# Query rows in seven units of 128, full-array scores and eleven value slots in an attention and maxout kernel

## The chip, the core and the metric

The kernel runs on one core of one Trainium2 chip. The metric is the device time of a whole execution, in microseconds (us). Of the core this text names TensorE (PE, its weight loads PEld), VectorE (DVE), ScalarE (ACT), GpSimd (POOL) and SyncE (SP). SP computes nothing here; it issues the DMAs, one after another and in program order.

## The reference

The inputs are q, k, v of shape (8, 12, 448, 64), that is 8 batches of 12 heads with 448 rows of 64, two gain vectors of 64, and four 768 x 768 weight matrices. All are float32 in the computation (the weights arrive as 64-bit floats, which the kernel decodes itself).

```python
def rmsnorm(x, g):
    rms = np.sqrt(np.mean(x * x, axis=-1, keepdims=True) + 1e-06)
    return x / rms * g
q_n, k_n = rmsnorm(q, g_q), rmsnorm(k, g_k)
scores = np.matmul(q_n, k_n.transpose(0, 1, 3, 2)) / np.sqrt(64)
attn = np.exp(scores - scores.max(-1, keepdims=True))
attn = attn / (attn.sum(-1, keepdims=True) + 1e-09)
x = np.matmul(attn, v)          # heads side by side: 3584 tokens x 768
h = np.maximum(np.maximum(x @ w1, x @ w2), x @ w3)
out = h @ w_out
```

## The kernel before

Work goes by pairs of heads: pair g of 48 holds two heads of one batch, six pairs make a batch. `beat(g, i)` is called with g from 0 to 48 and i from 0 to 11, so a pair has twelve beats, and each beat emits instructions of several stages for all engines. The order in which `beat` and what it calls emit them is the order in which each engine executes; nothing reorders them. Each emitted instruction waits on semaphores for its operands and buffers. An engine whose next instruction waits holds up all that is behind it.

The first six pairs (`PLAIN = 6`) are computed in float32. From pair 6 on each float32 operand of a product is split into an upper and a lower float16 part, and a product is three float16 products (upper by upper, upper by lower, lower by upper: `TERMS`).

A pair from 6 on goes through these steps:

- **Loads** (`load_q`, `load_k`, `load_v`; L332, L344 to L349), three pairs ahead for queries and keys (beats 0 and 1), six ahead for values (beat 5). Queries: 112 partitions, four rows of each head on a partition, one DMA for the pair. Keys and values: seven groups of 64 columns on 128 partitions, three of each head and one that holds the last 64 rows of one head on the lower half of the partitions and of the other head on the upper half; four DMAs for each of the two tensors.
- **Normalise** two pairs ahead: squares on POOL (L367), their sums on DVE (L374), power -0.5 on POOL (L388, L392), scale on POOL (L399, L411, L424, L428).
- **Split and transpose** one pair ahead: upper part on ACT (L439), lower on POOL (L445), then one DMA transpose each for keys and queries (`turn_rows`, L455): kt and qt have the head's 64 columns on partitions, head 0 on the lower half and head 1 on the upper.
- **Scores** (`scores`, L558): four query blocks of 112 rows (c = 0 to 3), each for both heads. A matmul has K = 64, one head on each half of the array's rows, so the two heads' matmuls run beside each other. Three terms make six matmuls of 448 columns in a block.
- **Softmax**: maximum over both heads in one DVE instruction (L569), exponential with sum on ACT for each head (L583), scaled upper part on ACT (L658), lower part on DVE (L668).
- **Transpose of the weights** (`turn_weights`, L678): one DMA transpose for each block into pt. The one of block 3 is emitted at beat 2 of the next pair, the others at beats 5, 8 and 11.
- **Weighted sum** (`add_values`, L706), at beat 7 of the next pair: output columns of the two heads on the two halves of the array, four groups of keys by three terms by two heads, 24 matmuls of 448 columns, which go by twos beside each other: 12 slots.

The plain pairs transpose on PE instead (`turn_whole` L468, `turn_plain` L605), so SP has only loads for them.

Between these, `thirds` feeds the feed-forward part of batches already attended to: 18 first-layer blocks of 18 matmuls of 448 columns (L735) and six or eight second-layer blocks of 18 matmuls of 384 columns (L799) for each batch. The quota of a beat (`THIRDS`) is fixed, so that one batch's feed-forward is spread over the next six pairs. That of the last batch runs after the last attention pair. Results are stored from SP (L774) by query block order: since four rows lie on a partition, a 128-token block is written in two pieces as a rule. The weights are loaded, decoded on DVE (L198, L202, L207) and split during the first twelve pairs or so.

Of the kernel before, what the change touches and what calls it, by code (L numbers as in the profile page):

```python
# [16 lines left out]
P = 128  # L17
# [22 lines left out]
def qknorm_attention_maxout_ffn_kernel(  # L40
# [41 lines left out]
    QP = S // NQ  # L82
# [51 lines left out]
    half_neg = const.tile([P, 15], F32, name="half_neg")  # L134
    nc.vector.memset(half_neg, -0.5)
    half = const.tile([P, 1], F32, name="half")
    nc.vector.memset(half, 0.5)

    sums = [const.tile([P, 15], F32, name=f"ss{i}") for i in range(2)]
    for t in sums:  # L140
        nc.vector.memset(t, 1.0)

    key_rows = [const.tile([P, 4, 2, D], F32, name=f"kn{i}") for i in range(2)]
    for t in key_rows:
        nc.gpsimd.memset(t[HALVES[1], 3, 0], 0.0)
        nc.gpsimd.memset(t[HALVES[0], 0, 1], 0.0)
# [181 lines left out]

    def load_q(g):
        b, pr = divmod(g, NP)  # L330
        qr = sb.tile([QP, 2, NQ, D], F32, name="qr", bufs=2)
        nc.sync.dma_start(  # L332
            out=qr,
            in_=q[b, 2 * pr:2 * pr + 2].rearrange("h (p c) d -> p h c d", c=NQ),
        )
        st.setdefault(g, {})["qr"] = qr


    def load_kv(g, name, src, bufs, on=(nc.sync, nc.sync)):
        b, pr = divmod(g, NP)  # L340
        t = sb.tile([P, 7, D], F32, name=name, bufs=bufs)
        rows = src[b, 2 * pr:2 * pr + 2]
        for h in range(2):
            on[h].dma_start(  # L344
                out=t[:, 4 * h:4 * h + 3],
                in_=rows[h, 0:3 * P].rearrange("(p c) d -> p c d", c=3),
            )
        on[0].dma_start(out=t[HALVES[0], 3], in_=rows[0, 3 * P:S])
        on[1].dma_start(out=t[HALVES[1], 3], in_=rows[1, 3 * P:S])  # L349
        st.setdefault(g, {})[name] = t  # L350

    def load_k(g):
        load_kv(g, "kr", k, 2, (nc.sync, nc.sync if g else nc.scalar))

    def load_v(g):
        load_kv(g, "vr", v, 8)


    def squares(g, what):
        s = st[g]  # L360
        src = s["kr"] if what == "k" else s["qr"].rearrange("p h c d -> p (h c) d")
        rows, n = src.shape[0], src.shape[1]
        sq = sb.tile([P, 8, D], F32, name="sq", tag="rows", bufs=3)[:rows, :n]
        if g < 2:
            nc.scalar.activation(sq, src, AF.Square)
        else:
            nc.gpsimd.tensor_tensor(out=sq, in0=src, in1=src, op=ALU.mult)  # L367
        s["sq" + what] = sq

    KQ = {"k": slice(0, 7), "q": slice(7, 15)}  # L370

    def sum_squares(g, what):
        sq = st[g].pop("sq" + what)
        nc.vector.tensor_reduce(  # L374
            sums[g % 2][:sq.shape[0], KQ[what]], sq, axis=AX, op=ALU.add
        )

    def inv_rms(g, what):
        s, at = st[g], KQ[what]
        if "ri" not in s:  # L380
            s["ri"] = sb.tile([P, 15], F32, name="ri", bufs=2).rearrange(
                "p (n o) -> p n o", o=1
            )
        ri = s["ri"][:, at, 0]
        by, eps = 1.0 / D, RMS_EPS
        if what == "k":
            by, eps = k_mean, k_eps
# [6 lines left out]
    def scale_q(g):  # L394
        s = st[g]
        qr, ri = s.pop("qr"), s.pop("ri")
        qn = sb.tile([QP, 4, 2, D], F32, name="qn", tag="rows", bufs=3)
        on = nc.gpsimd if g else nc.vector
        on.tensor_tensor(  # L399
            out=qn.rearrange("p c h d -> p h c d"),  # L400
            in0=qr,
            in1=ri[:QP, 7:].rearrange("p (h c) o -> p h c o", h=2).broadcast_to(
                [QP, 2, 4, D]
            ),
            op=ALU.mult,
        )
        s["qn"] = qn
        if g < PLAIN:
            return
        n = qn.rearrange("p c h d -> p (c h) d")  # L410
        nc.gpsimd.tensor_tensor(  # L411
            out=n, in0=n,
            in1=gain[:QP].rearrange("p (o d) -> p o d", o=1).broadcast_to([QP, 8, D]),
            op=ALU.mult,
        )

    def scale_k(g):
        s = st[g]
        kr, ri = s.pop("kr"), s["ri"]
        kn = key_rows[g % 2]  # L420
        on = nc.gpsimd if g else nc.vector
        for h, rows in enumerate(HALVES):
            own = slice(4 * h, 4 * h + 3)
            on.tensor_tensor(  # L424
                out=kn[:, h:h + 3, h], in0=kr[:, own],
                in1=ri[:, own].broadcast_to([P, 3, D]), op=ALU.mult,
            )
            on.tensor_tensor(  # L428
                out=kn[rows, 3 - 3 * h, h:h + 1], in0=kr[rows, 3:4],
                in1=ri[rows, 3:4].broadcast_to([64, 1, D]), op=ALU.mult,  # L430
            )
        s["kn"] = kn


    def upper_rows(g, what):
        s = st[g]
        n = s.pop(what + "n").rearrange("p c h d -> p (c h d)")
        parts = sb.tile([n.shape[0], 2, 4 * P], F16, name=what + "p", bufs=1)
        nc.scalar.copy(parts[:, 0], n)  # L439
        s[what + "p"] = parts, n  # L440

    def lower_rows(g, what):
# [3 lines left out]
            out=parts[:, 1], in0=n, in1=parts[:, 0], op=ALU.subtract  # L446
# [3 lines left out]
    def turn_rows(g, what):  # L450
        s = st[g]
        parts = s.pop(what + "p")
        rows = parts.shape[0]
        t = sb.tile([P, 2, 4, rows], F16, name=what + "t", bufs=2)
        nc.sync.dma_start_transpose(  # L455
# [630 lines left out]
```

## Time and profile before

| | us |
|---|---|
| median of three runs | 1091.29 (1090.59 to 1093.42) |
| the profiled execution | 1093.06 |
| its span, first to last instruction | 1091.2 |
| PE busy | 1008.7 (92%) |
| DVE, ACT, POOL busy | 760.4, 690.3, 714.8 |
| mean share of the DMA engines' time in use | 68.6% |

The profile is of one execution. Busy time of PE is that of pipelined matmuls whose ends are modelled, so a stretch of matmuls is read by the distance between starts. SP has no busy time on the page; its rows in the timeline (SPq) are the instructions that issue a DMA, and their length is how long the issue held SP, not how long the data took. "Landing" in the list of DMAs counts from the issue until the data is there. A merged row (x2, x3) runs from the first start to the last end and includes what lies between.

### The profile page before, as it was taken

Reading aid. Unit: us, or ns where it says so; the run is one execution under the profiler, and the core shown is the slowest. Engines: PE = TensorE matmul, PEld = TensorE weight load, DVE = VectorE, ACT = ScalarE, POOL = GpSimd, SP = SyncE. Lnnn points to the kernel's source line nnn. Section 1 sums busy time; section 2 is a strip of 40 time slices with the busy share of each in tenths; the row PEclk is TensorE's granted clock in tenths of the full one; section 3 lists DMA queues with packets and bytes.
Section 4 is the critical chain, followed back from the end, with each engine's and each line's share of the span. In section 5 each row is a group of like instructions: output and inputs, shape, how many; then the busy total and the mean of one; then the engine's idle time right before and its main releaser. Section 6 shows DMA issues by size and latency. Waiting matters only on the chain.

```text
span 1091.2 us, 18210 instructions
## 1 busy us (share of the span) xinstructions
PE 1008.7 (92%) x6168; PEld 497.0 (46%) x6168; DVE 760.4 (70%) x1395; ACT 690.3 (63%) x1575; POOL 714.8 (65%) x806
## 2 busy tenths in 40 slices
PE   3576868988899999999999999999999999999998
PEld 1333333434444454444544454444444554445555
DVE  3799998898767686786777767777686766761210
ACT  3488878757767576676766676667676676752001
POOL 5378898966777778677777776777777777610000
PEclk9698777999999999999999999999999999999999
DMA  4544458776798779888887798878877797653002
GB/s 127 172 144 155 146 152 177 163 146 124 156 174 146 145 156 177 155 154 139 177 150 145 142 169 173 152 138 160 173 151 137 142 183 137 112 98 73 1 1 58
DMA packets 426652, 152.27 MB, mean 140 GB/s; under 512 B 372928, under 2 KB 422336, under 8 KB 426560
## 3 DMA queue, kind: packets, MB, share of 16 engines
q1 hardware_dynamic: 425888, 150.75, 68.6%
q8 instruction: 48, 0.79, 0.3%
q10 hardware_dynamic: 672, 0.38, 0.1%
q14 instruction: 44, 0.36, 0.1%
HBM read 51.97 MB, written 11.01 MB: 58 GB/s over the span
## 4 chain that ended last, share of the span: by engine, by line
PE 69%; DVE 4%; ACT 2%; issue 2%; DVEq 0%; ACTq 0%
PE acc L735 37%; PE acc L799 14%; PE sc L558 9%; PE av L706 9%; DVE pp L668 2%; ACT pp L658 1%; DVE nm L569 1%; DVE wo_sb L314 0%; ACT xt L720 0%; ACT wo_sb L309 0%; DVE acc L749 0%; DVE ht L759 0%; DVE v_rows L172 0%; ACT ht L755 0%; ACT kp L439 0%
## 5 line engine op out<-in xcount | busy, mean ns | idle before, releaser
L735 PE MATMUL acc<-xt,w_sb 128*128 128x448 f16 x2592 | 518.4, 355 | 0.0
L735 PEld LDWEIGHTS <-w_sb 128*128 128x128 f16 x2592 | 244.6, 98 | 260.3 <-issue 49.8
L583 ACT ACTIVATE sc<-sc,nm 112x448 f32<-112x448 f32 x336 | 204.2, 608 | 191.0 <-DVE nm L569 184.4
L569 DVE TENSOR_REDUCE nm<-sc 112x2 f32<-112x896 f32 x192 | 208.2, 1084 | 94.2 <-PE sc L558 92.8
L658 ACT ACTIVATE pp<-sc,rs 112x448 f16<-112x448 f32 x336 | 195.1, 633 | 63.7 <-ACT sc L583 32.5
L668 DVE SCALAR_TENSOR_TENSOR pp<-sc,rs,pp 112x448 f16<-112x448 f32 x336 | 212.7, 674 | 1.6 <-ACT pp L658 1.6
L392 POOL TENSOR_TENSOR ri<-ri,half_neg 128x7 f32<-128x7 f32 x96 | 154.2, 1606 | 8.0
L558 PE MATMUL sc<-kt,qt 64*112 64x448 f16 x1008 | 132.2, 368 | 23.1 <-DVE pp L668 20.7
L799 PE MATMUL acc<-wo_sb,ht 128*128 128x384 f16 x864 | 149.2, 326 | 1.1 <-DVE ht L759 0.8
L764 POOL COPY hx<-ht 128x128 f16<-128x128 f16 x48 | 15.6, 325 | 178.8 <-DVE ht L759 171.7
L799 PEld LDWEIGHTS <-ht 128*128 128x128 f16 x864 | 81.2, 98 | 65.3 <-issue 11.8
L706 PE MATMUL av<-pt,vp 128*64 128x448 f16 x1008 | 108.3, 356 | 0.0
L558 PEld LDWEIGHTS <-qt 64*112 64x112 f16 x1008 | 53.4, 126 | 93.1 <-issue 59.4
L445 POOL TENSOR_TENSOR kp<-kn,kp 128x512 f16<-128x512 f32 x42 | 50.8, 1209 | 46.9 <-ACT kp L439 46.9
L721 DVE SCALAR_TENSOR_TENSOR xt<-av,xt 128x448 f16<-128x448 f32 x42 | 26.2, 624 | 70.6 <-ACT xt L720 70.6
L706 PEld LDWEIGHTS <-vp 128*64 128x64 f16 x1008 | 49.6, 108 | 55.7 <-issue 30.0
L536 POOL TENSOR_TENSOR vp<-vr,vp 128x448 f16<-128x448 f32 x42 | 43.9, 1045 | 39.0 <-ACT vp L530 38.9
L374 DVE TENSOR_REDUCE ss<-sq 128x7 f32<-128x448 f32 x96 | 61.1, 638 | 11.4 <-POOL sq L367 8.5
L445 POOL TENSOR_TENSOR qp<-qn,qp 112x512 f16<-112x512 f32 x42 | 48.6, 1157 | 22.0 <-ACT qp L439 22.0
L522 POOL TENSOR_SCALAR vr<-vr,v_up 128x448 f32<-128x448 f32 x42 | 59.6, 1420 | 0.0
L411 POOL TENSOR_TENSOR qn<-qn,gain 112x512 f32<-112x512 f32 x42 | 54.6, 1299 | 3.3
L399 POOL TENSOR_TENSOR qn<-qr,ri 112x512 f32<-112x512 f32 x47 | 53.6, 1140 | 3.2
(118 smaller groups left out, 1128.0 us busy)
## 6 DMA issues: line engine op xcount, KB each, us to landing
raw<-in_moe_w_dram SPq DMA_DIRECT2D x18, 768.0 KB, 4.4
qr<-in_q_dram SPq DMA_DIRECT2D x48, 224.0 KB, 3.0
vr<-in_v_dram SPq DMA_DIRECT2D x96, 96.0 KB, 2.6
kr<-in_k_dram SPq DMA_DIRECT2D x95, 96.0 KB, 3.0
raw<-in_moe_w_out_dram SPq DMA_DIRECT2D x6, 768.0 KB, 5.2
pt<-pp SPq DMA_TRANSPOSE x168, 4.1
out_dram<-osb SPq DMA_DIRECT2D x8, 336.0 KB, 3.3
out_dram<-osb SPq DMA_DIRECT2D x8, 288.0 KB, 3.8
```

The source lines that it names most:

```text
L374: nc.vector.tensor_reduce(sums[g % 2][:sq.shape[0], KQ[what]], sq, axis=AX, op=ALU.add)
L392: nc.gpsimd.tensor_tensor(out=ri, in0=ri, in1=half_neg[:, at], op=ALU.pow)
L445: nc.gpsimd.tensor_tensor(out=parts[:, 1], in0=n, in1=parts[:, 0], op=ALU.subtract)
L522: nc.gpsimd.tensor_scalar(out=vr, in0=vr, scalar1=v_up[:, g // NP:g // NP + 1], scalar2=None, op0=ALU.mult,)
L558: nc.tensor.matmul(sc[:QP, h, :S], qt[rows, qp, c], kt[rows, kp, KEYS[h]], start=n == 0, stop=n == len(TERMS) - 1,)
L569: nc.vector.tensor_reduce(nm, sc[:QP, :, :S], axis=AX, op=ALU.max, negate=True)
L583: nc.scalar.activation(to, sc[:QP, h, :S], AF.Exp, bias=nm[:, h:h + 1], accum_out=total,)
L658: nc.scalar.activation(pp[:, 0, h], sc[:QP, h, :S], AF.Copy, scale=rs[:, h:h + 1])
L668: nc.vector.scalar_tensor_tensor(out=pp[:, 1, h], in0=sc[:QP, h, :S], scalar=rs[:, h:h + 1], in1=pp[:, 0, h], op0=ALU.mult, op1=ALU.subtract,)
L706: nc.tensor.matmul(av[half, :S], vp[rows, group, vpart], pt[rows, 7 * wp + group], start=u == 0 and n == 0, stop=u == 3 and n == len(TERMS ...
L735: nc.tensor.matmul(acc[:, :S], wt[:, wp, c], xs[c][:, xp], start=(c == 0 and n == 0), stop=(c == NCT - 1 and n == 2),)
L799: nc.tensor.matmul(acc[:, :HW], lhs, wo_sb[:, f, wp, half * HW:(half + 1) * HW], start=(f == 0 and n == 0), stop=(f == NFT - 1 and n == 2),)
```

## The change

Queries are laid out like keys: seven units of 128 rows, six of one head each and one that has the last 64 rows of both heads. In the diff:

- Loads: queries come with four DMAs instead of one (two main ones with 256 bytes for each row, two of 64 partitions). Values come with seven instead of four, as the last group of the first head is written on both halves and the second head's rows are shifted by 64.
- Squares, sums, scales, upper and lower parts work on [128, 448] for queries and keys; scaling keys is one instruction instead of four.
- The upper and lower parts lie side by side in a unit's 128 columns, so that the transposed unit has the upper part on partitions 0 to 63 and the lower on 64 to 127. Keys are kept twice, the second time with the halves exchanged (`swap_keys`, two copies by DMA at beat 8). A score block is then two matmuls of K = 128 for each head: one by kt, one by the exchanged kt, which is the sum of upper by upper, lower by lower, and both mixed terms. Blocks 0 to 2 have 128 rows of each head (four matmuls). Block 3 has 64 rows of both heads in one bank, on the two column halves (four matmuls).
- Softmax, upper and lower weights: seven instructions of 128 rows a step instead of eight of 112; the lower weights are written in reversed groups of 64 keys.
- Transpose of the weights: three of 128 rows and two of 64 rows a pair, instead of four of 112. Upper and lower parts of 448 keys are one stretch of 896, which is seven blocks of 128; the middle block holds 64 keys of both parts.
- Weighted sum: 11 slots instead of 12. It needs a copy of the upper values with exchanged halves (`swap_values`, two copies by DMA at beat 3).
- In the plain pairs a unit is transposed by six PE instructions instead of four, and weights of a pair by 35 instead of 28.
- Stores write a 128-token block in one piece. At the start the preparation of the gains (`prep_gain`) comes behind the scaling of the first pair, and the plain pairs no longer need it for the keys.

```diff
     def load_rows(g, name, src, on):
+        t = sb.tile([P, UNITS, D], F32, name=name, bufs=2)
+        for h, half in enumerate(HALVES):
+            rows = src[b, 2 * pr + h]
+            first = LEFT * h
+            if name == "kr":
+                main = rows[first:first + 3 * P].rearrange("(p c) d -> p c d", c=3)
+            else:
+                main = rows[first:first + 3 * P].rearrange("(c p) d -> p c d", p=P)
+            units = slice(h, 6, 2) if g < PLAIN else slice(4 * h, 4 * h + 3)
+            on[h].dma_start(out=t[:, units], in_=main)
+            last = rows[0:LEFT] if h else rows[3 * P:S]
+            on[h].dma_start(out=t[half, rest(g)], in_=last)
...
     def load_v(g):
-        load_kv(g, "vr", v, 8)
+        t = sb.tile([P, 2, 4, D], F32, name="vr", bufs=7)
...
+        on.dma_start(
+            out=t[:, 0, 0:3], in_=rows[0:3 * P].rearrange("(p c) d -> p c d", c=3)
+        )
+        for half in HALVES:
+            on.dma_start(out=t[half, 0, 3], in_=rows[3 * P:S])
...
+        on.dma_start(out=t[lower, 1, 0], in_=rows[0:LEFT])
+        on.dma_start(out=t[upper, 1, 0:3], in_=main[lower])
+        on.dma_start(out=t[lower, 1, 1:4], in_=main[upper])
+        on.dma_start(out=t[upper, 1, 3], in_=main[upper, 2])
...
+    def swap_keys(g):
+        t = st[g]["ks"]
+        for to, of in (HALVES, HALVES[::-1]):
+            nc.sync.dma_start(out=t[to, 1], in_=t[of, 0])
...
+    def swap_values(g):
+        s = st[g]
+        s["vs"] = sb.tile([P, 8, D], F16, name="vs", bufs=2)
+        for to, of in (HALVES, HALVES[::-1]):
+            nc.sync.dma_start(out=s["vs"][to], in_=s["vp"][of, 0])
...
     def scores(g, c):
-        for n, (qp, kp) in enumerate(TERMS):
-            for h, rows in enumerate(HALVES):
-                nc.tensor.matmul(
-                    sc[:QP, h, :S], qt[rows, qp, c], kt[rows, kp, KEYS[h]],
-                    start=n == 0, stop=n == len(TERMS) - 1,
-                )
+        keys = (slice(0, S), slice(S, 2 * S))
+        if c < 3:
+            for h in range(2):
+                for n in range(2):
+                    nc.tensor.matmul(
+                        sc[:, h, :S], qt[:, 4 * h + c], kt[:, n, keys[h]],
+                        start=n == 0, stop=n == 1,
+                    )
+        else:
+            for n in range(2):
+                for h, rows in enumerate(HALVES):
+                    nc.tensor.matmul(
+                        sc[rows, 0, :S], qt[:, 3, rows], kt[:, n, keys[h]],
+                        start=n == 0, stop=n == 1,
+                    )
...
     def turn_weights(g, c):
+        if c < 3:
+            first = LEFT + c * P
+            nc.sync.dma_start_transpose(
+                out=pt[:, :, first:first + P], in_=pp.rearrange("p h k -> p (h k)")
+            )
+            return
+        for h, half in enumerate(HALVES):
+            first = 0 if h else LEFT + 3 * P
+            nc.sync.dma_start_transpose(
+                out=pt[:, 7 * h:7 * h + 7, first:first + LEFT], in_=pp[half, 0]
+            )
...
     def add_values(g):
+        steps = [(part, u, u) for u in range(4) for part in range(2)]
+        steps += [(2, 2 - i, 4 + i) for i in range(3)]
+        for n, (part, u, block) in enumerate(steps):
+            for h, half in enumerate(HALVES):
+                values = vs[:, 4 * h + u] if part == 2 else vp[:, part, 4 * h + u]
+                nc.tensor.matmul(
+                    av[half, :S], values, pt[:, 7 * h + block, SHIFT[h]:SHIFT[h] + S],
+                    start=n == 0, stop=n == len(steps) - 1,
+                )
...
     def beat(g, i):
+                if i == 8:
+                    swap_keys(g + 1)
...
+        if PLAIN <= w and i == 3:
+            swap_values(w)
```

How the change moves SP's work shows at two places of a middle pair. The first is SP from the key load of pair g + 3 at beat 0 to the transposes of the next pair's keys and queries at beats 4 and 5. kr and qr are loaded keys and queries, pt the transposed weights (from pp), kt and qt transposed keys and queries, vs the exchanged values (from vp). Before:

```order
L344 DMA kr<-in_k_dram 128x192 x2
L348 DMA kr<-in_k_dram 64x64
L349 DMA kr<-in_k_dram 64x64
L332 DMA qr<-in_q_dram 112x2x256
L678 DMA_TRANSPOSE pt<-pp 128x14x112
L455 DMA_TRANSPOSE kt<-kp 128x8x128
L455 DMA_TRANSPOSE qt<-qp 128x8x112
```

And now, the same stretch:

```order
L342 DMA kr<-in_k_dram 128x192
L344 DMA kr<-in_k_dram 64x64
L342 DMA kr<-in_k_dram 128x192
L344 DMA kr<-in_k_dram 64x64
L342 DMA qr<-in_q_dram 128x3x64
L344 DMA qr<-in_q_dram 64x64
L342 DMA qr<-in_q_dram 128x3x64
L344 DMA qr<-in_q_dram 64x64
L741 DMA_TRANSPOSE pt<-pp 128x7x64 x2
L558 DMA vs<-vp 64x512 x2
L450 DMA_TRANSPOSE kt<-kp 128x7x128
L450 DMA_TRANSPOSE qt<-qp 128x7x128
```

Eight issues have become fourteen: three more for queries, one more transpose of weights, two copies of values. The second place is SP from the value load at beat 5 to the last transpose of the pair's weights. Before:

```order
L344 DMA vr<-in_v_dram 128x192 x2
L348 DMA vr<-in_v_dram 64x64
L349 DMA vr<-in_v_dram 64x64
L678 DMA_TRANSPOSE pt<-pp 128x14x112 x3
```

And now:

```order
L360 DMA vr<-in_v_dram 128x192
L364 DMA vr<-in_v_dram 64x64 x2
L367 DMA vr<-in_v_dram 64x64
L368 DMA vr<-in_v_dram 64x192
L369 DMA vr<-in_v_dram 64x192
L370 DMA vr<-in_v_dram 64x64
L735 DMA_TRANSPOSE pt<-pp 128x14x128
L457 DMA kt<-kt 64x896 x2
L735 DMA_TRANSPOSE pt<-pp 128x14x128 x2
```

Seven issues have become twelve: three more for values, and two copies of the next pair's keys, which stand between the first and the second transpose of the weights.

More of the change, by code (lines that the diff above doesn't have):

```diff
@@ L133, in qknorm_attention_maxout_ffn_kernel @@
     nc.scalar.activation(warm, warm, AF.Exp)
-    half_neg = const.tile([P, 15], F32, name="half_neg")
+    half_neg = const.tile([P, 2 * UNITS], F32, name="half_neg")
     nc.vector.memset(half_neg, -0.5)
[L136 to L146, printed above, removed]
+    root = const.tile([P, 1], F32, name="root")
+    nc.vector.memset(root, 0.5)
+    sums = [const.tile([P, 2 * UNITS], F32, name=f"ss{i}") for i in range(2)]
     def largest(column, done, gaps):
@@ L405, in scale_q @@
             op=ALU.mult,
         )
-        s["qn"] = qn
-        if g < PLAIN:
+        if what == "k":
             return
[L410 to L421, printed above, removed]
-        for h, rows in enumerate(HALVES):
[L423 to L426, printed above, removed]
-            )
[L428 to L432, printed above, removed]
+        s.pop("ri")
@@ L879, in prep_gain @@
     def prep_gain():
-        nc.vector.tensor_tensor(out=gain, in0=gains[:, 0], in1=gains[:, 1], op=ALU.mult)
         row_largest(g_top[:, 0:1], gain)
@@ L913, in qknorm_attention_maxout_ffn_kernel @@
     inv_rms(0, "q")
-    scale_k(0)
-    scale_q(0)
+    nc.vector.tensor_tensor(out=gain, in0=gains[:, 0], in1=gains[:, 1], op=ALU.mult)
+    scale_rows(0, "k")
+    scale_rows(0, "q")
     column = ps_m.tile([P, 512], F32, name="column", tag="m")
```

323 lines of the change are left out of this document (169 added, 154 removed).

## Prediction

> **What bounds the kernel now.** I read the page first (busy shares, then the chain), then the windows by stage, then one pair's timeline on PE, then the same pair on SP with SP's waits, and last the DMA list of the steady stretch.
>
> ```profile
> PE 1008.7 (92%) x6168; PEld 497.0 (46%) x6168; DVE 760.4 (70%) x1395; ACT 690.3 (63%) x1575; POOL 714.8 (65%) x806
> PE 69%; DVE 4%; ACT 2%; issue 2%; DVEq 0%; ACTq 0%
> ```
>
> PE carries the chain. The windows (microseconds, then busy time of PE, PEld, DVE, ACT, POOL, granted clock, DMA share) show where it does not:
>
> ```profile
> 82.00:109.00 27.00, 17.89 (x100) 8.48 (x98) 26.54 (x30) 22.12 (x49) 23.94 (x18) 0.90 0.49 155
> 136.00:164.00 28.00, 17.76 (x101) 10.31 (x99) 26.23 (x38) 19.27 (x40) 26.82 (x22) 0.71 0.59 154
> 246.00:300.00 54.00, 46.88 (x316) 23.89 (x316) 43.96 (x87) 41.25 (x92) 39.03 (x46) 1.00 0.70 141
> 300.00:880.00 580.00, 576.21 (x3639) 280.07 (x3640) 422.04 (x830) 394.86 (x926) 428.42 (x506) 1.00 0.83 156
> 1000.00:1050.00 50.00, 50.00 (x269) 26.11 (x267) 8.15 (x13) 6.15 (x12) 1.18 (x4) 1.00 0.03 9
> ```
>
> Three stages, then. Up to about 300 us DVE (26.54 of 27) and POOL decide with PE idle a third of the time. From 300 to 880 PE is busy 576.21 of 580, at full clock. From about 1000 on only feed-forward is left. In the middle stage I look at PE:
>
> ```profile
> 604.68 0.78 PE L558 MATMUL sc<-kt,qt 64*112 64x448 f16 x6 [0.95 <-DVE pp L668]
> 605.39 2.44 PE L735 MATMUL acc<-xt,w_sb 128*128 128x448 f16 x12
> 607.77 2.58 PE L706 MATMUL av<-pt,vp 128*64 128x448 f16 x24
> 610.27 0.78 PE L558 MATMUL sc<-kt,qt 64*112 64x448 f16 x6
> 610.98 4.15 PE L735 MATMUL acc<-xt,w_sb 128*128 128x448 f16 x21
> 615.06 0.78 PE L558 MATMUL sc<-kt,qt 64*112 64x448 f16 x6
> ```
>
> From start to start, 21 matmuls on the whole array take 615.06 - 610.98 = 4.08 us, 0.194 each; the 24 of the weighted sum 2.50 us, that is 0.208 for a slot of two; six of the scores 0.71 us, that is three slots of 0.237. SP over the same pair, with the landing times behind it:
>
> ```profile
> 617.95 0.52 SPq L332 DMA_DIRECT2D qr<-in_q_dram  x1
> 619.80 1.46 SPq L678 DMA_TRANSPOSE pt<-pp  x1
> 621.75 1.34 SPq L455 DMA_TRANSPOSE kt<-kp  x1
> 623.75 1.22 SPq L455 DMA_TRANSPOSE qt<-qp  x1
> 625.03 1.06 SPq L344 DMA_DIRECT2D vr<-in_v_dram  x2
> 626.13 0.48 SPq L348 DMA_DIRECT2D vr<-in_v_dram  x1
> 626.65 0.59 SPq L349 DMA_DIRECT2D vr<-in_v_dram  x1
> 627.34 6.98 SPq L678 DMA_TRANSPOSE pt<-pp  x3
> 634.41 1.50 SPq L344 DMA_DIRECT2D kr<-in_k_dram  x2
> 635.96 0.48 SPq L348 DMA_DIRECT2D kr<-in_k_dram  x1
> 636.49 0.59 SPq L349 DMA_DIRECT2D kr<-in_k_dram  x1
> 637.18 1.00 SPq L774 DMA_DIRECT2D out_dram<-osb  x2
> ```
> ```profile
> 667.70 5.78 SPq L678 DMA_TRANSPOSE pt<-pp  x3
> 673.58 1.22 SPq L344 DMA_DIRECT2D kr<-in_k_dram  x1
> ```
> ```profile
> q1 hardware_dynamic: 287063, 89.50, 82.4%
> qr<-in_q_dram SPq DMA_DIRECT2D x30, 224.0 KB, 3.0
> pt<-pp SPq DMA_TRANSPOSE x120, 4.2
> vr<-in_v_dram SPq DMA_DIRECT2D x58, 16.0 KB, 2.1
> kt<-kp SPq DMA_TRANSPOSE x30, 3.6
> ```
>
> The last fence is of 300 to 880 us: 30 loads of queries in 580 us, so a pair takes 19.4 us (580 / 30, rounded up since the stretch begins and ends within pairs). An issue holds SP whatever it moves. Four value loads take 627.34 - 625.03 = 2.31 us, 0.58 each with the gap behind, and the 16 KB ones (0.48, 0.59) no less than the 96 KB ones (1.06 for two). A transpose holds it for 1.2 to 1.5 us (singles), up to 5.88 / 3 = 1.96 where three rows run together with waits.
>
> SP's bill for a pair before: nine loads and one store at 0.58 are 5.8; four weight transposes at 1.6, which I take between 1.46 and 1.96 and nearer the singles, 6.4; kt and qt at 1.35, 2.7; together 14.9 of 19.4 us. The other 4.5 are waits, of which the largest in that stretch is:
>
> ```profile
> SPq L678 <- DVE pp L668: 70.3, 51, 3.5
> ```
>
> So SP is 77% occupied, and its slack is what the change spends.
>
> **The change part by part.**
>
> *SP.* Of a pair the change makes 19 plain issues instead of nine: keys 4, queries 4, values 7, exchanged keys 2, exchanged values 2; stores fall to 0.7 a pair, since a block of tokens goes out in one piece. 19.7 x 0.58 = 11.4 us. Three large transposes: 3 x 1.6 = 4.8. Two small ones (64 rows, seven blocks): the trace has none, their ends are a plain issue (0.58) and a query transpose (1.28 from 623.75 to 625.03); since kt with 1,024 columns costs 1.34 and pt with 1,792 only 1.46, size counts for little, and I take 1.25 each, 2.5. kt and qt with seven blocks for eight: 2.7. Sum 21.4 us a pair, against 14.9, and against a period of 19.4. All 27 are on SP, and pt, kt and the exchanged copies are what PE waits for. The ends: plain issues at 0.53, large transposes at 1.46, small at 0.58, kt and qt at 1.22 give 10.4 + 4.4 + 1.2 + 2.4 = 18.4; large at 1.96, small at 1.28, kt and qt at 1.34 and 1.22, plain at 0.58 give 11.4 + 5.9 + 2.6 + 2.6 = 22.5.
>
> Does SP then set the pace without further waits? Its order helps: the exchanged keys stand behind qt, seven loads and a weight transpose, some 7 us after kt was issued, and kt lands in 3.6. The exchanged copy is issued at beat 8 at the earliest and read by the scores at beat 11; a plain 16 KB load lands in 2.1. When SP is behind, PE stalls there once a pair, and the weights that SP wants are finished by then. So I add nothing for waits: a period of 21.4, 2.0 more than before. Full bills hold while values are still loaded, which is up to pair 41; from 300 us on that is 30 pairs: 30 x 2.0 = +60 us.
>
> *PE.* Scores: three blocks of four whole-array matmuls, 12 x 0.194 = 2.33, and one block of two slots on column halves, 2 x 0.208 = 0.42; 2.75 against 4 x 0.71 = 2.84. Weighted sum: one slot of 0.208 less. Together -0.30 us a pair. This counts only where PE sets the pace, which in my forecast is the six pairs from 42 on: -2 us. If it counted everywhere it would be 42 x 0.30 = -13.
>
> *DVE, ACT, POOL* lose an eighth of the row work.
>
> ```profile
> L569 DVE TENSOR_REDUCE nm<-sc 112x2 f32<-112x896 f32 x192 | 208.2, 1084 | 94.2 <-PE sc L558 92.8
> L374 DVE TENSOR_REDUCE ss<-sq 112x8 f32<-112x512 f32 x48 | 32.6, 678 | 4.9 <-POOL sq L367 4.3
> L172 DVE TENSOR_REDUCE v_rows<-vr 128x1 f32<-128x448 f32 x48 | 29.2, 608 | 4.9 <-DMA vr<-in_v_dram 4.8
> ```
>
> In the plain stage DVE is full: a maximum over one bank for one over two saves about half of 1.08, the query sums 678 x 64/512 = 0.08, while the largest of v grows by 608 x 64/448 = 0.09. About -0.5 us for six pairs: -3 us. PE's added transposes lie in its idle third (17.89 of 27 busy). Pairs 6 to 11 have SP's bill as well as the decoding; I give them no gain (full cover would be worth about -1 us a pair on DVE, so -4 to -6).
>
> *The start.*
>
> ```profile
> 7.82 0.22 DVE L880 TENSOR_TENSOR gain<-gains 128x64 f32<-128x64 f32 x1 [6.75 <-DMA gains<-in_g_k_dram]
> 9.87 1.21 DVE L374 TENSOR_REDUCE ss<-sq 128x7 f32<-128x448 f32 x2
> ```
>
> The sums no longer wait for the gains' preparation (9.87), but the first queries come by three more issues (3 x 0.58 = 1.7 later) and the weights' first loads by six more. Between 0 and -5, I take -3.
>
> Sum against the profiled execution: 1093.1 + 60 - 2 - 3 - 3 = 1145. The median of the runs is 1.8 below that execution, so **1143 us**.
>
> **The Trainium skill against this.** "DMA: Bandwidth & Descriptors", section "Issuing engines are not separate DMA queues", says that the time a sequencer takes to start a DMA is usually small beside the DMA itself. Here it is not: 1.34 of 3.6 us for kt, 0.59 of 2.1 for a small load, in one queue that holds 27 of them a pair. By that rule the bill would not bind, and the time would be that of rival A. The same page's "Rules for kernel authors" advises one transfer of 128 partitions instead of two for the halves; the rows agree, and every copy that the change adds is of halves.
>
> **Rivals.**
>
> A, faster: SP's bill fits. It decides at a bill of 19.1 us (19.4 - 0.3), which the lowest rows allow (18.4). For it: SP's waits of 4.5 us vanish in a full queue, and no kt or pt is late now. Against it: all of the cheapest rows would have to hold at once. Then the gains of PE count: 1093.1 - 13 - 3 - 3 - 5 = 1069, as a median **1067**. Chance 0.15.
>
> B, about the same: the bill is 19.5 and gains and stalls cancel, 30 x 0.3 = 9 against 10: **1091**. Chance 0.05.
>
> C, slower by the DMA engines and not by issuing. 82.4% of 16 x 580 us for 287063 packets is 26.6 ns a packet; a pair needs 0.824 x 19.4 = 16.0 us of all engines. The change adds 672 packets for queries (896 of 256 bytes for 224 of 1,024), 128 for values, 256 for the copies: 1,056 x 26.6 / 16 = 1.8 us. At 17.8 us they fit, but unevenly; with bursts the period could be 20.5: 1093.1 + 30 x 1.1 - 8 = 1118, median **1116**. Chance 0.10. SP would show long landings and waits for DMAs.
>
> D, slower still: PE's stalls lower its clock. The row 136 to 164 us has PE busy 17.76 of 28 at 0.71. Against it: 246 to 300 us has it busy 46.88 of 54 at 1.00, which is more idle than I forecast (2 in 21). By "TensorE: Matmul & The Clock Gate", section "What's actually happening", the clock halves after an idle window of about 3.4 us; one stall of some 2 us a pair would not reach that, and if it did, 3.4 us at half speed would cost 1.7 a pair. From rows alone: at 0.9 (82 to 109 us) PE's 19.1 would take 21.2, no more than SP's bill, so it hardly adds; at 0.71, 27 us. Chance 0.03 and left out of the range.
>
> **How the numbers follow.** The forecast (SP's bill, 1143) has the rest, 0.67; its own range is 1108 (20.3 a pair) to 1176 (22.5). The range to hold eight in ten takes in B and C, and on the high side 0.5 us a pair for waits that I set at nothing: 1085 to 1190. A and D and the outer tail are left out. About 3 us can be told from no change here (0.3%). Slower: 0.67 + 0.10 + 0.03 = 0.80; A 0.15; the same 0.05.
>
> **What the changed profile would show.** Right: in 300 to 880 us SPq rows follow each other with hardly a gap; PE's busy share falls to about nine tenths; PE's idle time there is ahead of the first score block, ended by the DMA of kt, or ahead of the weighted sum, ended by pt; the pairs up to 41 are about 21.4 us apart, and the last six under 19.4; weighted sums of 22 matmuls take 2.3 us and score groups of four 0.78. Wrong: periods under 19.4 with PE full (A); small transposes at half a microsecond; SP waiting for DMAs (C); PEclk under 1.00 after 300 us (D).

## The result, and the profile after

| | before | after |
|---|---|---|
| median, us | 1091.67 (4 runs, 1090.59 to 1093.42) | 1279.32 (4 runs, 1278.32 to 1281.43) |
| span of the profiled execution, us | 1091.2 | 1277.6 |
| mean granted clock in it | 0.968 | 0.915 |

The ratio is 1.172 (95% interval 1.1698 to 1.1742). Slower was forecast, but 1143; the time is above the whole range, so the loss is 3.6 times the one that was worked out.

From the page after, the busy time of the engines and the groups that wait longest:

```profile
PE 1054.4 (83%) x5850; PEld 545.4 (43%) x5850; DVE 712.9 (56%) x1348; ACT 640.1 (50%) x1437; POOL 615.5 (48%) x661
L584 PE MATMUL sc<-kt,qt 128*128 128x448 f16 x504 | 136.8, 386 | 164.9 <-DMA kt<-kt 158.3
L708 ACT ACTIVATE pp<-sc,rs 128x448 f16<-128x448 f32 x294 | 173.0, 634 | 227.8 <-DMA pt<-pp 183.9
```

DVE, ACT and POOL are all less busy than before, in microseconds and in share. PE waits 158.3 us for `kt<-kt`, the exchanged copy of the keys. ACT waits 183.9 us until a weight transpose has freed a buffer. Both are DMAs that SP issues.

Where the time went is read from the weighted sums. That of pair 6 starts at 201.7 us (189.8 before), that of pair 11 at 322.2 (294.7), that of pair 41 at 1069.3 (881.3), that of pair 47 at 1182.7 (996.0). So the start and the plain pairs cost 11.9, pairs 6 to 11 15.6, the 30 pairs that follow 160.5; the last six give 1.3 back, and feed-forward alone at the end 0.3. The sum, 186.4, is the difference of the spans. Windows of after, in the prediction's columns:

```profile
322.00:1069.00 747.00, 613.78 (x3375) 307.61 (x3376) 401.48 (x807) 363.49 (x846) 374.54 (x422) 0.91 0.70 137
1069.00:1183.00 114.00, 111.62 (x673) 58.38 (x672) 66.48 (x136) 65.33 (x151) 47.79 (x56) 0.99 0.77 145
```

In the middle stage a pair takes 747 / 30 = 24.9 us. No computing engine is full (PE 613.78 of 747), and the DMA share is 0.70 where it was 0.83. As soon as the loads of values have ended, PE is full again (111.62 of 114). The queue that is full in between is SP's. One pair of it, from the first load of keys to the next:

```profile
661.01 1.02 SPq L342 DMA_DIRECT2D kr<-in_k_dram  x1
662.08 0.50 SPq L344 DMA_DIRECT2D kr<-in_k_dram  x1
662.63 0.58 SPq L342 DMA_DIRECT2D kr<-in_k_dram  x1
663.25 0.49 SPq L344 DMA_DIRECT2D kr<-in_k_dram  x1
663.84 0.53 SPq L342 DMA_DIRECT2D qr<-in_q_dram  x1
...
666.19 2.52 SPq L741 DMA_TRANSPOSE pt<-pp  x2
668.81 1.17 SPq L558 DMA_DIRECT2D vs<-vp  x2
670.09 1.24 SPq L450 DMA_TRANSPOSE kt<-kp  x1
671.43 2.03 SPq L450 DMA_TRANSPOSE qt<-qp  x1
673.51 0.58 SPq L360 DMA_DIRECT2D vr<-in_v_dram  x1
674.14 1.14 SPq L364 DMA_DIRECT2D vr<-in_v_dram  x2
675.33 0.59 SPq L367 DMA_DIRECT2D vr<-in_v_dram  x1
...
677.95 1.53 SPq L735 DMA_TRANSPOSE pt<-pp  x1
679.53 1.76 SPq L457 DMA_DIRECT2D kt<-kt  x2
681.72 3.70 SPq L735 DMA_TRANSPOSE pt<-pp  x2
685.52 1.03 SPq L342 DMA_DIRECT2D kr<-in_k_dram  x1
```

Each row begins some 0.05 to 0.1 us behind the end of the one before, with one hole of 0.4 (681.29 to 681.72): but for that hole the pair of 24.5 us is issuing and these short gaps. In the rows of before the holes were 0.5 to 1.3 us, ahead of each of the three single transposes. What PE makes of it, from its timeline and its waits between 322 and 1069 us (total, times, longest):

```profile
629.01 0.35 PE L584 MATMUL sc<-kt,qt 128*128 128x448 f16 x1
633.91 1.30 PE L584 MATMUL sc<-kt,qt 128*128 128x448 f16 x3 [4.54 <-DMA kt<-kt]
```
```profile
PE sc L584 <- DMA kt<-kt: 128.8, 30, 7.8
```

The first matmul of the first score block, which takes kt itself, runs; the next stands 4.54 us until the exchanged copy is there. It is one stall a pair, 30 in 30 pairs, 4.3 us each.

### The profile page after: what moved, and what is told of

It reads as the page before. It is cut to its first block, busy times and chain, and to the rows that moved or that the text cites. A ratio compares the mean times of both kernels' runs of the same rounds, so it can differ in the third digit from the quotient of the medians.

```text
span 1277.6 us, 18009 instructions
## 1 busy us (share of the span) xinstructions
PE 1054.4 (83%) x5850; PEld 545.4 (43%) x5850; DVE 712.9 (56%) x1348; ACT 640.1 (50%) x1437; POOL 615.5 (48%) x661
## 5 line engine op out<-in xcount | busy, mean ns | idle before, releaser
L796 PEld LDWEIGHTS <-w_sb 128*128 128x128 f16 x2592 | 263.3, 103 | 273.8 <-issue 65.2
L622 ACT ACTIVATE sc<-sc,nm 128x448 f32<-128x448 f32 x294 | 178.8, 608 | 238.8 <-DVE nm L606 234.1
L708 ACT ACTIVATE pp<-sc,rs 128x448 f16<-128x448 f32 x294 | 173.0, 634 | 227.8 <-DMA pt<-pp 183.9
L606 DVE TENSOR_REDUCE nm<-sc 128x2 f32<-128x896 f32 x192 | 186.7, 973 | 165.9 <-PE sc L584 94.5
L584 PE MATMUL sc<-kt,qt 128*128 128x448 f16 x504 | 136.8, 386 | 164.9 <-DMA kt<-kt 158.3
L719 DVE SCALAR_TENSOR_TENSOR pp<-sc,rs,pp 128x448 f16<-128x448 f32 x294 | 188.0, 676 | 1.7 <-ACT pp L708 1.7
L825 POOL COPY hx<-ht 128x128 f16<-128x128 f16 x48 | 15.6, 325 | 271.5 <-DVE ht L820 271.5
L584 PEld LDWEIGHTS <-qt 128*128 128x128 f16 x504 | 48.2, 102 | 222.4 <-DMA kt<-kt 172.7
L548 POOL TENSOR_TENSOR vp<-vr,vp 128x512 f16<-128x512 f32 x42 | 49.2, 1172 | 168.8 <-ACT vp L542 168.8
L856 PEld LDWEIGHTS <-ht 128*128 128x128 f16 x864 | 86.1, 101 | 65.2 <-issue 13.7
L165 DVE TENSOR_REDUCE v_rows<-vr 128x1 f32<-128x512 f32 x48 | 32.8, 684 | 114.9 <-DMA vr<-in_v_dram 114.9
L782 DVE SCALAR_TENSOR_TENSOR xt<-av,xt 128x448 f16<-128x448 f32 x42 | 26.2, 624 | 91.8 <-ACT xt L781 91.7
L767 PE MATMUL av<-pt,vp 128*64 128x448 f16 x672 | 74.0, 360 | 3.5 <-DMA qr<-in_q_dram 1.8
L436 POOL TENSOR_TENSOR kp<-kn,kp 128x448 f16<-128x448 f32 x42 | 45.6, 1085 | 60.9 <-ACT kp L430 60.7
L436 POOL TENSOR_TENSOR qp<-qn,qp 128x448 f16<-128x448 f32 x42 | 43.5, 1036 | 26.6 <-ACT qp L430 23.4
```

The lines of the kernel that those rows point to most:

```text
L436: nc.gpsimd.tensor_tensor(out=parts[:, :, 1], in0=n, in1=parts[:, :, 0], op=ALU.subtract)
L548: nc.gpsimd.tensor_tensor(out=vp[:, 1], in0=vr.rearrange("p h n d -> p (h n) d"), in1=vp[:, 0], op=ALU.subtract,)
L584: nc.tensor.matmul(sc[:, h, :S], qt[:, 4 * h + c], kt[:, n, keys[h]], start=n == 0, stop=n == 1,)
L606: nc.vector.tensor_reduce(nm[:, :n], sc[:, :n, :S], axis=AX, op=ALU.max, negate=True)
L622: nc.scalar.activation(to, sc[:, h, :S], AF.Exp, bias=nm[:, h:h + 1], accum_out=total,)
L708: nc.scalar.activation(pp[:, h, :S], sc[:, h, :S], AF.Copy, scale=rs[:, h:h + 1])
```

## The experiments

The theory, called I, is the prediction's: the time for which SP is held by issuing sets the pace, 0.6 us for each extra issue, whatever it moves. Its rivals T and C put it on the transfers and not on their issue: the DMA engines' time (T), and the landing of the copies that PE waits for (C; these letters are not those of the prediction, whose C is T here). Another is that the new layout of scores and weighted sums itself costs the time. V came up on the way: the first reader of the values, DVE, sets it. All times of before on the same chips are 1089.49 or 1089.64. One run each, except where several rounds are named.

**More issues in the kernel before.** Twelve loads a pair on SP, 64 partitions of 128 bytes each, into a tile that nothing reads; pairs 6 to 41.

```diff
+        if PLAIN <= g < G - 6 and i in (0, 5):
+            more_loads(g, 6, 3 * (i // 5))
```

> The kernel before, with twelve more loads issued by SP in each of the pairs 6 to 41 (64 partitions of 128 bytes, into a tile that nobody reads), and no other part of the change. Theory I (issuing: what SP's DMAs cost in issue time sets the pace of a pair): SP's bill goes from about 16.5 us a pair, as the two traces now show it, to 16.5 + 12 x 0.63 = 24 us, over the 19.4 that PE needs; 36 pairs x 4.6 = +165 us, about 1255 us. Theory T (transfers: the 16 DMA engines set the pace): 768 small packets a pair are 1 us more of engine time on 16 us, under 19.4, so no change: 1091 to 1100 us. Theory C (chain: PE waits for the round trip of the exchanged copies, a latency): there are no copies here, no change: 1091 us.

Measured: 1288.93, 34 more than expected: the pairs from 11 to 41 take 24.65 us where 24 were worked out. Rows of SP and the middle stage of this run:

```profile
607.61 1.52 SPq L344 DMA_DIRECT2D kr<-in_k_dram  x2
609.18 0.48 SPq L348 DMA_DIRECT2D kr<-in_k_dram  x1
609.70 0.59 SPq L349 DMA_DIRECT2D kr<-in_k_dram  x1
610.34 3.79 SPq L363 DMA_DIRECT2D extra<-in_v_dram  x6
```
```profile
322.00:1000.00 678.00, 562.66 (x3240) 264.55 (x3241) 377.62 (x740) 351.53 (x827) 376.67 (x445) 0.92 0.64 123
```

Small loads alone turn the old kernel into something as slow as the new one, with the same picture: SP without holes, PE at 562.66 of 678, clock 0.92, DMA engines at 0.64. Six of them hold SP for 3.79 + 0.09 us, 0.65 each. That issuing can cost this much is shown; that it is what costs it in the changed kernel needs the other direction.

**Three more issues in the kernel before.** The same edit with `i == 5` and three loads; three rounds.

> The kernel before with three more small loads issued by SP in each of the pairs 6 to 41 (twelve made it 1289 us). Theory I with a threshold: SP's bill 16.9 + 3 x 0.65 = 18.9 us, still under PE's 19.4, so at most a few us: 1091 to 1100 us. If every issue cost its time whatever the slack: 36 x 2.0 = +70 us, 1160 us.

Measured: 1110.54, ratio 1.0177 (1.0153 to 1.0202). Three issues are 1.95 us a pair, which would be 70 us over 36 pairs if none were hidden. Some 21 appeared: from pair 11 to 41 most pairs stay near 19.4, two take 24.5 and 25.8, and three 21.4 to 21.8. Both expectations were off: the threshold is there, as the smaller one had it, but the slack below it isn't smooth.

**The copies from another engine.** The changed kernel with its four half copies issued by POOL:

```diff
-            nc.sync.dma_start(out=t[to, 1], in_=t[of, 0])
+            nc.gpsimd.dma_start(out=t[to, 1], in_=t[of, 0])
...
-            nc.sync.dma_start(out=s["vs"][to], in_=s["vp"][of, 0])
+            nc.gpsimd.dma_start(out=s["vs"][to], in_=s["vp"][of, 0])
```

> The changed kernel with the four exchanged copies of a pair issued by POOL instead of SP. Theory I: SP loses four issues, 2.4 us net (the issue behind a large transpose pays its tail of 0.5 whoever it is), 24.8 to 22.4; 36 x 2.4 = -86 us, about 1190 us, if POOL's own issue does not hold up its other work. Theory C: the copies are issued no earlier and land later, so PE's wait for them stays or grows: 1279 us or more. Theory T: 1279 us.

Measured: 1194.96. The same bytes go through the same DMA engines, and 84.4 us are gone: over 36 pairs and four issues 0.59 an issue. The pairs from 11 to 41 take 22.4 us, as the bill has it, and PE stands 10.7 us in the whole run for the exchanged copies, where it stood 158.3. Their landing is only 0.5 us shorter (2.3 us instead of 2.8), while a pair is 2.5 us shorter. By T and C nothing should have changed.

**Fewer loads.** The changed kernel with rows in their natural order, so that from pair 6 on one DMA brings the queries of both heads, one the keys, four the values: 6 issues where the change has 15. The same bytes in 1,024 more packets a pair.

```diff
+        if g >= PLAIN:
+            rows = src[b, 2 * pr:2 * pr + 2].rearrange("h s d -> (h s) d")
+            nc.sync.dma_start(out=t, in_=rows.rearrange("(c p) d -> p c d", p=P))
+            st.setdefault(g, {})[name] = t
+            return
...
+        for h in range(2):
+            nc.sync.dma_start(
+                out=t[:, h, 0:3],
+                in_=rows[h, 0:3 * P].rearrange("(c p) d -> p c d", p=P),
+            )
...
+            nc.sync.dma_start(
+                out=t[half, :, 3], in_=rows[:, 3 * P:S].rearrange("h p d -> p h d")
+            )
```

> The changed kernel with rows in natural order: from pair 6 on queries come by one DMA and keys by one (seven units of 128 rows are contiguous), values of all pairs by four instead of seven. Nine issues of a pair less on SP, but 1,024 more packets, since every row is now a packet of 256 bytes. Theory I: the bill falls by 9 x 0.62 = 5.6 to 19.2 us, near what PE needs (18.6 in the last pairs of the changed kernel): 36 x 5.6 = -200 us, about 1080 us. Theory T: 1,024 x 22 ns / 16 = 1.4 us more a pair: 1310 us or more. Theory C: 1279 us.

Measured: 1087.24, all of the loss back, although the DMA engines have a little more to do: 17.9 us of their time a pair (0.91 of 19.7 us) against 17.4 in the changed kernel (0.70 of 24.9). Its middle stage:

```profile
300.00:870.00 570.00, 545.94 (x3281) 284.07 (x3282) 386.23 (x781) 349.62 (x816) 360.83 (x407) 1.00 0.91 172
```

A DMA share of 0.91 with a shorter time refutes T and C for the changed kernel, where it is 0.70. The new scores, softmax, transposes and weighted sums are all in this run, so the layout itself doesn't cost the time either. The clock is at 1.00 again. SP's rows still fill the 19.7 us of a pair, where the expected bill was 19.2, so issuing still sets the pace here.

**Fewer loads, and the copies on POOL.** Both edits; three rounds.

> The kernel of fewer loads, with the four exchanged copies of a pair issued by POOL as well. SP's rows fill a whole pair there (19.1 to 19.6 us) and PE needs 18.6. Theory I: four issues less are 2.4 us, SP's bill 16.7, PE sets the pace: 30 pairs x 1.0 and a little in the pairs 6 to 11, about 1055 us. Theory T (the 16 DMA engines, at a share of 0.91 in the kernel of fewer loads): the same packets, 1087 us.

Measured: 1077.96 (1076.59 to 1079.49), ratio to before 0.9884 (0.9863 to 0.9905). That is 1.2% less than before, small but clear of the noise. It misses the 1055 expected. The middle stage, and SP in one of the long pairs:

```profile
300.00:870.00 570.00, 555.83 (x3344) 290.49 (x3342) 392.61 (x796) 358.08 (x833) 431.38 (x533) 1.00 0.98 175
```
```profile
599.59 0.60 SPq L366 DMA_DIRECT2D vr<-in_v_dram  x1
600.29 9.04 SPq L733 DMA_TRANSPOSE pt<-pp  x3
609.43 0.54 SPq L336 DMA_DIRECT2D kr<-in_k_dram  x1
610.07 0.51 SPq L336 DMA_DIRECT2D qr<-in_q_dram  x1
```

The DMA engines are at 0.98 of their time. Most pairs take 18.6 to 18.7 us, others 19.2 to 20.9 and two 22.4 and 23.1. The three large weight transposes take 9.04 in this pair; over the stage one holds SP for 2.39 us on the mean, where it was 1.66 before, 1.82 in the changed kernel and 1.86 with fewer loads. SP's bill is no longer full, since 1.5 us of a pair are waits and holes, and the next limit is close behind it. That this limit is the DMA engines is argued from their share, not tested. The 1,024 packets explain only 0.5 us of it: the engines' time of a pair is 16.2 us before (0.83 of 19.5), 17.4 in the changed kernel, 17.9 with fewer loads and 19.0 here (0.98 of 19.4). Why the same bytes take 1.1 more here is open.

**Values from ACT.** The changed kernel with the seven loads of values on ACT:

```diff
-        on = nc.sync
+        on = nc.scalar
```

> The changed kernel with the seven value loads of a pair issued by ACT instead of SP. Theory I: SP's bill falls by 7 x 0.64 = 4.5 us from 24.8 to 20.3 us a pair, while ACT has 4.2 more on 13.3; 36 pairs x 4.5 = -160 us, about 1115 us. Theory T: the same packets on the same engines, 1279 us. Theory C: the copies are where they were, 1279 us. If PE's lower clock were the cause (theory H), 1279 us as well.

Measured: 1217.14, 102 later than expected. SP is relieved, but the work behind the loads on ACT is not. Waits of this run from 322 to 1000 us:

```profile
DVE rs L701 <- ACT sc L622: 201.0, 92, 8.1
ACT sc L622 <- DMA vr<-in_v_dram: 116.9, 19, 8.8
```

The exponential (L622) stands behind the loads for up to 8.8 us, and DVE behind the exponential: one full queue traded for another.

**Values from ACT, spread.** The same, but two loads a beat, and the reader of the values (`largest_v`) three beats later.

```diff
+            later(n // 2, load)
...
-            later(4, lambda: largest_v(g + 6))
+            later(7, lambda: largest_v(g + 6))
```

> The changed kernel with its seven value loads issued by ACT, now two to a beat instead of seven in a row (in a row they took 1217 us where 1115 was expected), and the largest value taken seven beats after instead of four. Theory I with a queue on ACT: seven issues in a row held ACT for 5 to 6 us and the softmax behind it; two at a time hold it for about one, so SP's bill of 20.3 us sets the pace: about 1120 us. If issues on ACT cost as much as on SP wherever they stand, since both use one descriptor generator: 1217 us.

Measured: 1139.16, where 1120 and 1217 were the two sides. So 78 of the 102 us of excess were not the number of issues on ACT. How much of them was the block of seven and how much the earlier reading of the values is not separated, since both changed; some 19 us more than expected stay.

**Fewer loads, with the values on POOL.** The four value loads of the version with fewer loads, on POOL.

```diff
-            nc.sync.dma_start(
+            nc.gpsimd.dma_start(
```

> The kernel of fewer loads, with the four value loads of a pair issued by POOL, the exchanged copies left on SP. Theory I: 4 x 0.65 = 2.6 us less on SP, 16.5 us, so PE sets the pace: about 1055 us. Theory T: 1087 us. Theory C (round trip of the exchanged copies): they stay where they were, 1087 us.

Measured: 1173.46: slower by 86 than with the same loads on SP. From its waits:

```profile
DVE v_rows L165 <- DMA vr<-in_v_dram: 164.8, 46, 6.4
ACT pp L706 <- DVE rs L703: 127.9, 22, 8.3
```

DVE's maximum of the values (L165) is emitted four beats behind the load. On POOL the issue comes later, DVE stands, and the reciprocal that ACT waits for is queued behind it. This is theory V: perhaps the same had slowed the changed kernel itself, whose page has a wait of 114.9 us in that place. Two runs decide.

**The same, with the maximum later.**

```diff
-            later(4, lambda: largest_v(g + 6))
+            later(7, lambda: largest_v(g + 6))
```

> The kernel of fewer loads with its value loads issued by POOL (which took 1173 us), with one edit: the largest value of a pair (DVE) is taken seven beats after the load is emitted instead of four. Theory V (DVE, in order, stood behind values that POOL issued late; DVE's rows show 165 us of waits for them): those waits go, SP's bill is 16.5 us, PE or the DMA engines set the pace: about 1080 us. If POOL's own issuing was the cause (each load holds POOL up), it stays near 1170 us.

Measured: 1105.73. V is right for this run: three beats took 68 us off, and the wait fell from 164.8 to 23.1. The remainder to 1080 stays unexplained.

**The changed kernel, with the maximum later.** The same line, in the kernel of the change.

> The changed kernel with the largest value taken seven beats after the load instead of four, nothing else. Theory I: DVE waits less for values (115 us of waits in the changed kernel), but SP's bill is the same, so no gain: 1270 to 1285 us. Theory V (what slows the changed kernel is DVE standing behind late values, not SP's queue): most of it comes back, under 1200 us.

Measured: 1279.60. Its waits:

```profile
PE sc L584 <- DMA kt<-kt: 156.1, 40, 8.8
DVE v_rows L165 <- DMA vr<-in_v_dram: 20.8, 6, 5.0
```

Ninety-four microseconds of DVE's waiting for values are gone, and not one of the time; DVE stands elsewhere instead (its wait for ACT's first part of `xt` grew from 91.7 to 195.8 us). V is rejected for the changed kernel: DVE waited because everybody did.

**Score groups cut in two.** To price what the change had saved on PE: the kernel before, with each group of six score matmuls cut into two and four by three feed-forward matmuls. The number of matmuls is as before.

```diff
-                scores(*divmod(k + 1, 4))
+                scores(*divmod(k + 1, 4), (0,))
+                thirds(1)
+                owed[0] -= 1
+                scores(*divmod(k + 1, 4), (1, 2))
```

> The kernel before with each group of six score matmuls cut into two and four, and three matmuls of the feed-forward put between them; the same matmuls in all. If a change between whole-array and half-row matmuls costs 93 ns each way, as the distances between starts in the trace have it (282 ns for 189), eight more changes a pair are 0.75 us: 42 x 0.75 = +31 us, about 1121 us. If the distance is only how the profile models the ends, 1090 us.

Measured: 1138.26, 48.6 above before and 17 more than the higher of the two expectations. On PE's timeline:

```profile
613.35 0.40 PE L561 MATMUL sc<-kt,qt 64*112 64x448 f16 x2
613.68 0.74 PE L738 MATMUL acc<-xt,w_sb 128*128 128x448 f16 x3
614.35 0.59 PE L561 MATMUL sc<-kt,qt 64*112 64x448 f16 x4
614.87 3.58 PE L738 MATMUL acc<-xt,w_sb 128*128 128x448 f16 x18
```

From 613.35 to 614.87 the nine matmuls take 1.52 us. Uncut, six of scores took 0.71 and three of feed-forward 3 x 0.194 = 0.58, together 1.29. Two more changes between half-row and whole-array matmuls cost 0.23, so over 0.1 us each. Four cuts a pair are 0.92, and the period rose from 19.4 to 20.4. By the mere number of matmuls there should have been no change. So the cost is real and not one of how ends are modelled, and somewhat above the 93 ns each.

## Why the prediction was wrong

**SP's bill, the step that failed.** The mechanism stood: SP's queue sets the pace, and one stall a pair falls before the first score block, ended by the kt copy. The size did not: "Sum 21.4 us a pair" measured 24.9. All SP rows from 322 to 1069 us, each with the gap ahead of it, divided by 30 pairs. A column made in this way always adds up to the period; it is a bill here because SP has next to no hole, as the excess of all gaps over 0.12 us is only 0.07 us a pair:

| | forecast, us a pair | measured |
|---|---|---|
| 15 loads | 8.7 | 9.8 |
| 4 half copies | 2.3 | 3.0 |
| 0.7 stores | 0.4 | 0.45 |
| three large transposes | 4.8 | 5.55 |
| two small transposes | 2.5 | 2.6 |
| kt and qt | 2.7 | 2.8 |
| instructions that only wait on a semaphore | 0 | 0.76 |
| sum | 21.4 | 24.9 |

Small terms and an omitted one, all times 30. They could have been read from before. First, 0.58 an issue came from the value loads, which follow the transpose of the queries and not a large one. The prediction quoted `kr x2` with 1.50 behind a block of large transposes and `vr x2` with 1.06, and used only the cheaper row. After, a load of keys takes 1.02 behind the large transpose and 0.58 otherwise, and two kt copies behind one take 1.76 where two vs copies take 1.17. Second, most added issues are pieces of 64 partitions: 0.59 and the gap, 0.64. Third, large transposes were priced "nearer the singles" (1.6, measured 1.85). Fourth, the waiting instructions themselves have 0.02 us and a gap of 0.05 each, nearly ten a pair. The bill of before, read from its rows with holes and waits left out, was 16.9 and not 14.9, so that the slack which the change spends was 2.6 of 19.5 us and not 4.5. The first point, its cause and its split from the others are read from rows; no run isolates them.

**"30 pairs x 2.0 = +60".** It measured 160.5. The excess over 19.4 is small against the bill, so an error of a sixth in the bill (3.5 of 21.4) makes an error of nearly two thirds in the loss. That is the arithmetic to note: where a queue goes from just under full to over full, the loss is a difference of two large numbers, and its range must come from the error of the whole bill. The prediction's upper end (22.5) moved only prices that differed between its rows, and not the count of what it had left out. One of its sums is off by 2 beside that: 20.3 us a pair gives 1110 and not 1108.

**"I add nothing for waits".** Right: SP has next to no hole, and the 0.76 a pair of the waiting instructions is the time they take with nothing left to wait for. The stalls on PE are SP's lateness, not an addition to it.

**The stage before 300 us.** "I give them no gain", -3 and -3 became +27.5. The bill governs pairs 6 to 11 as well: 21.0 us a pair became 24.1. The prediction had said that they "have SP's bill as well as the decoding", but it set the period of before as the floor and did not set 21.4 against it, which would have been +0.4 a pair.

The loss up to pair 6 lies wholly in the first pair: the first weighted sum starts at 65.2 us instead of 51.7, and from there to pair 6 the changed kernel is 1.6 us faster (the forecast gain of the plain pairs was 3). PE stands there for the largest of the first batch's values; the waits of after and of before from 30 to 170 us:

```profile
PE most L517 <- DVE v_most L510: 15.0, 2, 13.7
PE most L505 <- DVE v_most L498: 7.9, 2, 5.7
```

The values of six pairs must have come by then, with seven loads each instead of four: SP issues those of pairs 1 to 5 from 24.9 to 49.2 us, before from 26.1 to 37.8. With four loads a pair (the run with fewer loads) the first sum starts at 54.5. So "the start", put at -3 with only query and weight loads counted, is SP's queue again, and its step left out the value loads.

**PE's saving.** "-0.30 us a pair" was too small. Four of the last pairs run at 18.6 instead of 19.4, that is 0.8. From PE's timeline of after, in the last stage:

```profile
1084.73 0.92 PE L584 MATMUL sc<-kt,qt 128*128 128x448 f16 x4
1085.48 2.43 PE L796 MATMUL acc<-xt,w_sb 128*128 128x448 f16 x12
1087.85 1.71 PE L767 MATMUL av<-pt,vp 128*64 128x448 f16 x16
1089.38 0.73 PE L767 MATMUL av<-pt,vs 128*64 128x448 f16 x6
1089.95 0.55 PE L591 MATMUL sc<-kt,qt 128*64 128x448 f16 x4
```

A score group takes 0.75, four times 0.188, and the weighted sum 2.10 (2.3 forecast), 0.191 a slot. What was counted as slow slots (0.237 and 0.208) were slots of nearly the usual length plus changes between matmuls on halves of the array (rows or columns) and on the whole, or between two kinds of halves. Before has ten such changes a pair, and the change leaves two, into the weighted sum and out of the last score block: its four matmuls are two slots, 0.38, and take 0.48 until the next start. Eight changes at some 0.1 are nearly all of the 0.8, and cutting score groups adds eight to before at such a price (0.92). The Trainium skill, "TensorEngine Tiling (Array Packing)", section "Key Properties", says that switching modes requires a drain; the trace agrees and gives it a price here, about 0.1 us. For the sum it hardly counted: the saving applies where PE sets the pace, and the last six pairs gave -1.3 where -2 was forecast. That this is so near is luck: the saving of a pair was more than twice the forecast one, and one of the six pairs still took 22.8 us.

**The rivals.** A and B (the bill fits, or nearly) fell with the bill of the middle stage. C (the DMA engines) is refuted by the run with fewer loads. Its sum was near all the same, 17.8 us of the engines' time a pair where 17.4 were measured, and the engines seem to be the limit once issues are cheap (0.98). D named 1.00 as the test, and the clock did fall to 0.91. But it also fell to 0.92 with nothing added but small loads, and rose to 1.00 when issues went, with the new matmuls in place: it follows PE's idling and nothing waits for it while SP's queue is full. The prediction let the clock alone because it expected stalls of some 2 us. The stalls measured 4.3, and by the rule in the Trainium skill's "TensorE: Matmul & The Clock Gate", section "What's actually happening", which puts the idle window at about 3.4 us, a lower clock is then to be expected; the trace agrees (0.91).

**The rule on issue time.** The Trainium skill's "DMA: Bandwidth & Descriptors", section "Issuing engines are not separate DMA queues", calls the saving from issuing on several engines usually small, beside the time of the DMA. The measurement decides otherwise for this kernel: four of 27 issues moved from SP to POOL are worth 84.4 us of 1279. But its other half, that all of them run on the same 16 DMA engines, fits the fastest version, which has these engines at 0.98.

## What to carry to other kernels

Add up the issuing queue as you would an engine: each DMA's hold, with its gap, what follows a long transpose, and the waiting instructions, against the period of the steady stage; if the sum is near the period, trust it no further than a sixth. Merge loads before moving them: fewer issues returned the whole loss, while another engine's queue returned a part of it, and least where that engine's own work stood behind the issues. Look at the start of a kernel in the same way: 10.7 of the 13.5 us lost there came back with fewer value loads, and no steady stage shows them. A wait that shows up after a change (here DVE's 114.9 us) proves nothing until it is taken away and the time follows.

## What the runs showed of the hardware that was not expected

- An issue right behind a large DMA transpose (14 blocks of 128) holds SP for about 0.5 us longer: 1.02 instead of 0.58 for a load of keys. Why is open.
- A piece of 64 partitions with 128 bytes each costs SP 0.65 us with its gap, as much as one with 768 bytes. Size didn't count, number did.
- Changing between matmuls on half of the array's rows and on the whole array costs about 0.1 us each way; from column halves to the whole array it is the same (0.48 us for two slots of 0.19).
- With the DMA engines at 0.98 of their time, a large transpose holds SP longer, 2.39 us on the mean against 1.86 at 0.91 and 1.66 in the kernel before. It looks like a queue that pushes back, but was not tested by itself.
